# Softmax of phi taken where its tokens lie along a row, and brought to rows by way of DRAM

## The chip, the cores and the metric

One core of one Trainium2 chip. The metric is device microseconds of the whole program, inputs and output in DRAM. The five engines that the profile names are PE (TensorE; PEld is its weight load), DVE (VectorE), ACT (ScalarE), POOL (GpSimd) and SP (SyncE), which here only issues transfers.

## The reference

Attention through 32 memory slots per head, and behind it a mixer with a product over tokens and one over channels. Eight batches, eight heads, 576 tokens, 64 channels per head, 32 slots.

```python
# attention: q, k, v (8, 8, 576, 64), phi (8, 8, 576, 32)
a = np.exp(phi - np.max(phi, axis=2, keepdims=True))       # over the 576 tokens
a = a / (np.sum(a, axis=2, keepdims=True) + 1e-09)
k_m = np.einsum('bhsm,bhsd->bhmd', a, k)
v_m = np.einsum('bhsm,bhsd->bhmd', a, v)
scores = np.matmul(q, k_m.transpose(0, 1, 3, 2)) / np.sqrt(64)
scores = scores - np.max(scores, axis=-1, keepdims=True)    # over the 32 slots
attn = np.exp(scores)
attn = attn / (np.sum(attn, axis=-1, keepdims=True) + 1e-09)
x = np.matmul(attn, v_m)                                    # to (8, 576, 512)
# mixer: w_tok1 (576, 256), w_tok2 (256, 576), w_ch1 (512, 1536), w_ch2 (1536, 512)
u = x + (np.maximum(x.transpose(0, 2, 1) @ w_tok1, 0) @ w_tok2).transpose(0, 2, 1)
out = u + np.maximum(u @ w_ch1, 0) @ w_ch2
```

## The kernel before

Products whose result must stay exact split each float32 operand into a high and a low part and use three matmuls (high by high, high by low, low by high). ACT makes the high part with a copy, DVE or POOL the low part with a subtraction.

The work has two kinds of unit. A *quad* is four heads of one batch (16 of them, each attention and token mixing). A *chunk* is 512 tokens of u, through both channel products (cp and acc in the rows). The first three chunks are taken straight from PSUM; the u of later tokens is spilled to DRAM and done at the end in pairs of chunks with fewer products of sums.

The program runs in three stages, which the trace shows: to about 120 us the weights are converted and the first quads done, from 120 to 372 us the quads of batches 2 to 7 with chunks 1 and 2 between them, from 372 us the pairs. The stage in the middle is ordered by a planner: every step of every quad is entered with its engine, an estimated duration, the buffers that it takes and the steps that it waits for, and beside it stands a table of ranks, `PLACES`, one number for each step, that says which step goes first where several could. `plan` walks through this and writes one order, in which the instructions then stand on each engine. Its three numbers in the call (slack, margin, behind) and the due times in `do(...)` shape it too. The order of the last stage is written out in code.

Eleven quads, (2,1) to (7,1), are of the class `LateQuad`. In the kernel before, one goes like this. `load_turned` brings phi with a partition for each head and slot and the tokens along the row (288 KB). `phi_max` (L637) takes the largest of each row and turns these 128 numbers with a small transpose; `max_out` (L642) puts them into DRAM. `load_phi` (L621) brings phi a second time, now with a partition for each token (320 KB, padded to 640 columns); `max_in` (L648) reads the maxima back, spread over all partitions (tile r). `phi_sub` (L652) subtracts them on POOL, and `phi_only_exp` (L443) takes the exponential on ACT. `get_kv` (L662) calls `step_kv` (L446): 40 matmuls of phi by keys and values into the tile kvp, 130 columns each, since k and v carry a column of ones for the sums. `scales` (L665) adds 1e-9 to that column and takes the reciprocal. Then `spread_T`, `turn_T`, `get_kb` make the keys ready, and `scores` (rows with L490) needs them and q (L631). Softmax over slots follows; S goes to DRAM and comes back by rows (L542, then L552 and L554, tiles rows and side), is multiplied with the token weights (Ap), split into Ah and Al (L741, L745), multiplied with v (Rp, L753), and the result gives u (L772). ACT copies u to the tile side (L782), SP spills it (L800).

SP takes its instructions in order and issues nearly all transfers; a transfer whose buffer isn't free or whose data isn't there holds up all behind it. Of the rooms that matter there are one each for kv and q, two for phi and two for the turned phi, so the next quad's q can be issued only when the scores before have read the old one.

Beside the quads, the middle stage makes sums of weights for the pairs (L316, L317, L320), reads back the u of the first spilled chunks (tile u_p, L207) and makes its parts (L274, L278: xphi, xS, xkv), and adds up o, the residual of a chunk, on POOL (L179), which is stored to out (L188).

Of the kernel before, what the change touches and what calls it, by code (L numbers as in the profile page):

```python
# [28 lines left out]
def kernel(  # L29
# [20 lines left out]
    B, _, _, _, NC, _, D1 = kv.shape  # L50
    D = D1 - 1
# [369 lines left out]
    def kv_room(name):  # L421
        t = sb.tile([P, 2624], F32, tag="kv", name=name, bufs=1)[:, : 2 * NC * 4 * D1]
        return t.rearrange("p (z j i d) -> p z j i d", z=2, j=NC, i=4)

    class Quad:
        def __init__(s, b, Q):
            s.b, s.Q, s.n = b, Q, f"_{b}_{Q}"

# [28 lines left out]

        def scales(s):
            s.ms = wp.tile([P, 6], F32, tag="ms", name="ms" + s.n, bufs=1)
            sm = wp.tile([P, 1], F32, tag="ps", name="ps" + s.n, bufs=3)  # L460
            nc.vector.tensor_scalar_add(out=sm, in0=s.kvp[:, D:D1], scalar1=1e-9)
            nc.vector.reciprocal(out=sm, in_=sm)
            nc.vector.tensor_scalar_mul(out=s.ms, in0=mask[:, :6], scalar1=sm)
            s.per = sm

        def double_T(s):

            s.T = sb.tile([P, 2, D], F32, tag="pr", name="T" + s.n, bufs=2)
            nc.vector.tensor_scalar_mul(
                out=s.T, in0=s.kvp[:, :D].unsqueeze(1).to_broadcast([P, 2, D]), scalar1=s.per  # L470
            )
# [2093 lines left out]
```

## Time and profile before

| | |
|---|---|
| median of 3 runs | 721.87 us (721.57 to 722.58) |
| profiled execution | 722.28 us, of which its span is 720.4 us |
| PE, DVE, ACT, POOL busy in the span | 706.0, 519.6, 370.4, 82.6 us |
| mean granted clock of TensorE | 0.998 |
| DMA | 155.26 MB, 216 GB/s over the span; written to HBM 37.16 MB |
| chain that ended last | PE 89%, DMA 5%, DVE 3%, ACT 1%, issue 1% |

The busy times overlap: they are shares of one span. The chain is what stood between the start and the last instruction, step by step; an engine's share of it is what would shorten the run at once if it went. The granted clock is in parts of full speed.

### The profile page before, as it was taken

Reading aid. Unit: us, or ns where it says so; the run is one execution under the profiler, and the core shown is the slowest. Engines: PE = TensorE matmul, PEld = TensorE weight load, DVE = VectorE, ACT = ScalarE, POOL = GpSimd, SP = SyncE. Lnnn points to the kernel's source line nnn. Section 1 sums busy time; section 2 is a strip of 40 time slices with the busy share of each in tenths; the row PEclk is TensorE's granted clock in tenths of the full one; section 3 lists DMA queues with packets and bytes.
Section 4 is the critical chain, followed back from the end, with each engine's and each line's share of the span. In section 5 each row is a group of like instructions: output and inputs, shape, how many; then the busy total and the mean of one; then the engine's idle time right before and its main releaser. Section 6 shows DMA issues by size and latency. Waiting matters only on the chain.

```text
span 720.4 us, 11496 instructions
## 1 busy us (share of the span) xinstructions
PE 706.0 (98%) x4305; PEld 589.9 (82%) x4305; DVE 519.6 (72%) x857; ACT 370.4 (51%) x686; POOL 82.6 (11%) x79
## 2 busy tenths in 40 slices
PE   8899999999999989999999999999999999999998
PEld 8678888778888858888878888888888888888887
DVE  5999974887767877579785758966247977426983
ACT  6899774334545435554643465434345443436450
POOL 2132114111201411211400000000000000000000
PEclk9999999999999999999999999999999999999999
DMA  9975431988677998855726886185659064668302
GB/s 358 415 294 212 147 123 44 327 291 290 211 234 228 324 317 266 328 175 161 247 66 236 285 281 247 36 300 160 203 167 331 31 221 162 203 202 279 102 29 88
DMA packets 65503, 155.26 MB, mean 216 GB/s; under 512 B 10536, under 2 KB 28584, under 8 KB 61096
## 3 DMA queue, kind: packets, MB, share of 16 engines
q1 hardware_dynamic: 54936, 121.37, 47.9%
q10 hardware_dynamic: 10512, 33.17, 14.4%
q8 instruction: 34, 0.56, 0.3%
q14 instruction: 21, 0.17, 0.1%
HBM read 117.34 MB, written 37.16 MB: 214 GB/s over the span
## 4 chain that ended last, share of the span: by engine, by line
PE 89%; DMA 5%; DVE 3%; ACT 1%; issue 1%; SPq 0%; ACTq 0%; DVEq 0%
PE ma L291 14%; PE cp L145 13%; PE acc L168 12%; PE mU L2347 10%; PE mB L2347 7%; PE mc L291 7%; PE u L772 7%; PE mD L2347 3%; PE mA L2347 3%; PE mb L291 3%; PE Ap L572 3%; DMA raww<-in_w_tok_dram 2%; PE kvp L450 2%; DMA spilled<-side 2%; DMA side<-rows 1%; PE u L588 1%
## 5 line engine op out<-in xcount | busy, mean ns | idle before, releaser
L168 PE MATMUL acc<-hh,c 128*128 128x512 f32 x288 | 102.7, 401 | 0.0
L168 PEld LDWEIGHTS acc<-hh,c 128*128 128x128 f32 x288 | 54.6, 190 | 15.0 <-issue 4.2
L168 PE MATMUL acc<-hl,c 128*128 128x512 f32 x144 | 56.7, 394 | 0.0
L145 PE MATMUL cp<-uh,c1h 128*128 128x512 f32 x144 | 51.8, 400 | 0.0
L145 PE MATMUL cp<-ul,c1h 128*128 128x512 f32 x144 | 50.4, 391 | 0.0
L145 PE MATMUL cp<-uh,c1l 128*128 128x512 f32 x144 | 50.4, 391 | 0.0
L2333 ACT CAST rT<-hid 128x512 fp32r<-128x512 f32 x54 | 32.0, 621 | 26.8 <-PE mB L2347 15.6
L2334 DVE TENSOR_TENSOR rT<-hid,rT 128x512 fp32r<-128x512 f32 x54 | 35.6, 683 | 7.0 <-ACT rT L2333 7.0
L2201 DVE TENSOR_TENSOR hid<-mb,hid 128x512 f32<-128x512 f32 x12 | 8.3, 692 | 41.8 <-ACT hid L2281 41.8
L118 DVE SCALAR_TENSOR_TENSOR hl<-cp,hh 128x512 fp32r<-128x512 f32 x36 | 24.7, 686 | 18.1 <-ACT hh L115 18.1
L115 ACT ACTIVATE hh<-cp 128x512 fp32r<-128x512 f32 x36 | 21.6, 599 | 27.0 <-PE cp L145 26.5
L715 POOL TENSOR_TENSOR nat<-side,nat 128x512 fp32r<-128x512 f32 (+1 forms) x24 | 21.9, 911 | 98.2 <-ACT nat L706 72.5
L2204 ACT ACTIVATE hid<-hid 128x512 f32<-128x512 f32 x24 | 15.2, 632 | 34.8 <-DVE hid L2201 34.8
L145 PEld LDWEIGHTS cp<-uh,c1h 128*128 128x128 f32 x144 | 26.7, 188 | 6.4 <-issue 1.5
L145 PEld LDWEIGHTS cp<-uh,c1l 128*128 128x128 f32 x144 | 27.0, 188 | 5.9
L145 PEld LDWEIGHTS cp<-ul,c1h 128*128 128x128 f32 x144 | 27.1, 188 | 4.9
L168 PEld LDWEIGHTS acc<-hl,c 128*128 128x128 f32 x144 | 27.4, 190 | 4.1
L2333 ACT CAST r<-hid 128x512 fp32r<-128x512 f32 x36 | 22.4, 623 | 14.8 <-PE mU L2347 5.4
L2334 DVE TENSOR_TENSOR r<-hid,r 128x512 fp32r<-128x512 f32 x36 | 24.7, 685 | 4.5 <-ACT r L2333 4.2
L653 POOL TENSOR_TENSOR phi<-phi,r 128x640 f32<-128x640 f32 x11 | 17.8, 1617 | 86.4 <-DMA r<-top 70.5
L772 PE MATMUL u<-w2h,Rh 128*128 128x288 f32 x96 | 27.2, 298 | 0.3 <-ACT side L782 0.3
L291 PE MATMUL ma<-xrest_p,unit 128*128 128x512 f32 x108 | 27.4, 389 | 0.0
(380 smaller groups left out, 1914.7 us busy)
## 6 DMA issues: line engine op xcount, KB each, us to landing
unit<-sums ACTq DMA_DIRECT2D x54, 512.0 KB, 6.1
kv<-in_kv_dram SPq DMA_DIRECT2D x12, 1300.0 KB, 7.7
rawc<-in_w_ch_dram SPq DMA_DIRECT2D x12, 1024.0 KB, 8.2
q<-in_q_dram SPq DMA_DIRECT2D x16, 576.0 KB, 5.9
sums<-sums SPq DMA_DIRECT2D x12, 512.0 KB, 7.3
u_p<-spilled SPq DMA_DIRECT2D x6, 1024.0 KB
phi<-in_phi_dram SPq DMA_DIRECT2D x16, 320.0 KB, 3.4
unit<-sums ACTq DMA_DIRECT2D x18, 256.0 KB, 4.1
```

Of the source, the lines that this page charges most:

```text
L115: nc.scalar.activation(out=h, in_=ps, func=AF.Relu)
L118: nc.vector.scalar_tensor_tensor(out=l, in0=ps, scalar=0.0, in1=f32(h), op0=ALU.max, op1=ALU.subtract)
L145: nc.tensor.matmul(ps, l[:, a], r[:, a], start=n == 0, stop=n == len(mm) - 1)
L168: nc.tensor.matmul(ps, l_[f // 2][:, f % 2, a * P : (a + 1) * P], r[:, w], start=f == start and x == 0, stop=f == end - 1 and x == 2,)
L291: nc.tensor.matmul(ps, l, r, start=first and n == 0, stop=n == len(mm) - 1, skip_group_check=not first,)
L572: nc.tensor.matmul(ps[:, :TT], a, w, start=x == 0, stop=x == len(mm) - 1)
L653: eng.tensor_tensor(out=s.pt, in0=s.pt, in1=s.r.rearrange("p (i m) -> p i m", i=4) .unsqueeze(2) .to_broadcast([P, 4, NC, M]), op=ALU.subt ...
L715: eng.tensor_tensor(out=o, in0=a, in1=f32(h), op=ALU.subtract)
L772: nc.tensor.matmul(s.up[db, hf][:, :HALF], a, r, start=x == 0, stop=x == len(mm) - 1)
L2333: nc.scalar.copy(out=t[:, 0], in_=x)
L2334: nc.vector.tensor_tensor(out=t[:, 1], in0=x, in1=f32(t[:, 0]), op=ALU.subtract)
L2347: nc.tensor.matmul(s.banks[room][a][:, w], l_[:, a * P : a * P + P], r_, start=not (p or x) and name in ("11", "T1", "21", "T4"), stop=p = ...
```

## The change

For the eleven late quads phi is now loaded once, in the turned form, and the softmax is taken there. `phi_max` takes the largest of each row and negates it (one DVE instruction, no transpose). `phi_exp` on ACT takes the exponential with that number as its bias, and sums each row as it goes. `scales` adds 1e-9 to the sum and takes the reciprocal, now ahead of the product. `phi_turn` transposes the 128x576 tile on DVE in blocks of 32x32, `phi_out` puts it into DRAM (tile turns), `phi_in` brings it back with a partition for each token, in six transfers, in the way the rows of S come back (four of 64 KB, two of 16 KB). `get_kv` now uses 128 columns, takes the 64 tokens of the rest first, and kv has no column of ones (1,280 KB for 1,300). The second load of phi, the trip of the maxima and the subtraction on POOL are gone. On the host, tokens are laid out so that the blocks of 32 end at the right partitions. The table of ranks and the three numbers of the call are others, and so are the due times of these steps; the order of the whole middle stage changes with that.

```diff
-        t = sb.tile([P, 2624], F32, tag="kv", name=name, bufs=1)[:, : 2 * NC * 4 * D1]
+        t = sb.tile([P, 2624], F32, tag="kv", name=name, bufs=1)[:, : 2 * NC * 4 * D]
...
-        def phi_only_exp(s):
-            nc.scalar.activation(out=s.pt, in_=s.pt, func=AF.Exp)
-
-        def step_kv(s, ps=None):
-            s.kvp = bank([P, CW], "kvp" + s.n) if ps is None else ps
-            for j in range(NC):
-                for i in range(4):
-                    nc.tensor.matmul(
-                        s.kvp[32 * i : 32 * i + 32, : 2 * D1],
-                        s.pt[:, i, j, :],
-                        s.kv[:, :, j, i, :],
-                        start=j == 0,
-                        stop=j == NC - 1,
-                    )
...
-        def take_rows(s, t):
-            n, by_token = FULL * P, s.rows.rearrange("(i t) n -> t i n", t=32)
+        def by_rows(s, rows, t):
+            n, by_token = FULL * P, rows.rearrange("(i t) n -> t i n", t=32)
             main = t[:, :n].rearrange("p (i n) -> p i n", i=4)
             last = t[:TAIL, n:].rearrange("p (i m) -> p i m", i=4)
             for g in range(4):
@@ -554,6 +519,10 @@
                 nc.sync.dma_start(
                     out=last[32 * g : 32 * g + 32], in_=by_token[:, :, n + M * g : n + M * g + M]
                 )
+            return main, last
+
+        def take_rows(s, t):
+            main, last = s.by_rows(s.rows, t)
...
         def phi_max(s):
-            t = s.turned
-            nc.vector.tensor_reduce(out=t[:, :1], in_=t, axis=AX.X, op=ALU.max)
-            nc.vector.transpose(out=t[:, M : 2 * M], in_=t[:, :M])
-
-        def max_out(s):
-            s.top = dram.tile([1, 4 * M], F32, name="top" + s.n, tag="maxima", bufs=4)
-            nc.sync.dma_start(
-                out=s.top.rearrange("a (i m) -> (a i) m", m=M), in_=s.turned[:: P // 4, M : 2 * M]
-            )
-
-        def max_in(s):
-            s.r = sb.tile([P, 4 * M], F32, tag="pr", name="r" + s.n, bufs=2)
-            nc.sync.dma_start(out=s.r, in_=s.top.to_broadcast([P, 4 * M]))
-
-        def phi_sub(s, eng):
-            eng.tensor_tensor(
-                out=s.pt,
-                in0=s.pt,
-                in1=s.r.rearrange("p (i m) -> p i m", i=4)
-                .unsqueeze(2)
-                .to_broadcast([P, 4, NC, M]),
-                op=ALU.subtract,
-            )
+            s.col = wp.tile([P, 2], F32, tag="ps", name="col" + s.n, bufs=3)
+            nc.vector.tensor_reduce(out=s.col[:, :1], in_=s.turned, axis=AX.X, op=ALU.max, negate=True)
+
+        def phi_exp(s):
+            nc.scalar.activation(
+                out=s.turned, in_=s.turned, func=AF.Exp, bias=s.col[:, :1], accum_out=s.col[:, 1:]
+            )
+
+        def scales(s):
+            s.per = s.col[:, 1:]
+            nc.vector.tensor_scalar_add(out=s.per, in0=s.per, scalar1=1e-9)
+            nc.vector.reciprocal(out=s.per, in_=s.per)
+
+        def phi_turn(s):
+            s.pt = sb.tile([P, 4 * M * NC], F32, tag="phi", name="phi" + s.n, bufs=2)
+            nc.vector.transpose(out=s.pt[:, :S], in_=s.turned)
+
+        def phi_out(s):
+            s.turns = dram.tile([P, S], F32, name="turns" + s.n, tag="turns", bufs=2)
+            nc.sync.dma_start(out=s.turns, in_=s.pt[:, :S])
+
+        def phi_in(s):
+            s.pm, s.pl = s.by_rows(s.turns, s.pt)
 
         def get_kv(s):
-            s.step_kv(pch.tile([P, CW], F32, tag="ch", name="kvp" + s.n, bufs=2))
-
-        def scales(s):
-            s.per = wp.tile([P, 1], F32, tag="ps", name="ps" + s.n, bufs=3)
-            nc.vector.tensor_scalar_add(out=s.per, in0=s.kvp[:, D:D1], scalar1=1e-9)
-            nc.vector.reciprocal(out=s.per, in_=s.per)
+            s.kvp = pch.tile([P, CW], F32, tag="ch", name="kvp" + s.n, bufs=2)
+            for j in (FULL, *range(FULL)):
+                for i in range(4):
+                    own = s.pm[:, i, M * j : M * j + M] if j < FULL else s.pl[:, i]
+                    nc.tensor.matmul(
+                        s.kvp[M * i : M * i + M, : 2 * D], own, s.kv[: own.shape[0], :, j, i, :],
+                        start=j == FULL, stop=j == FULL - 1,
+                    )
 
         def vb_room(s, room):
             s.vb = side[0][:, 640:896] if room.tag[0] == "s" else sb.tile([P, 256], F32, tag="vb", name="vb" + s.n, bufs=1)
 
         def spread_v(s, room):
             s.vb_room(room)
-            EarlyQuad.spread_values(s, s.vb, s.kvp[:, D1 : D1 + D])
+            EarlyQuad.spread_values(s, s.vb, s.kvp[:, D : 2 * D])
...
-    ahead = [(quads[1, 0].x_u[3].end, late[1].load_turned)] + [(118.0, fn) for fn in (late[1].phi_max, late[1].max_out)]
+    ahead = [(quads[1, 0].x_u[3].end, late[1].load_turned)] + [(118.0, late[1].phi_max)]
...
-            turned = room("al", 2)
+            turned, col = room("al", 2), room("ps", 3)
             y = qd.l_turned = do(TURN_AT, "SP", 0.45, qd.load_turned, begin, take=[turned], move=0.81)
-            y = do(-38, "DVE", 0.85, qd.phi_max, y, use=[turned])
-            y = do(-37, "SP", 0.45, qd.max_out, y, use=[turned], move=0.02)
-            y.lands = True
-        z = do(-32, "SP", 0.45, qd.load_phi, begin, take=[phi_room], move=0.9)
-        r = room("pr", 2)
-        y = do(-30, "SP", 0.45, qd.max_in, y, z, take=[r], move=0.24)
-        z = do(-23, *PHI_SUB(qd), y, z, use=[phi_room, r], port=True)
-        e = do(-22, "ACT", 0.8, qd.phi_only_exp, z, use=[phi_room])
-        e.cushion = 2.0 * CUSHION
+            y = do(-40, "DVE", 0.72, qd.phi_max, y, take=[col], use=[turned])
+        z = do(-38, "ACT", 0.8, qd.phi_exp, y, use=[turned, col])
+        qd.scaled, qd.colr = do(-36, "DVE", 0.36, qd.scales, z, use=[col]), col
+        z = do(-37, "DVE", 0.8, qd.phi_turn, z, take=[phi_room], use=[turned])
+        z = do(-36, "SP", 0.45, qd.phi_out, z, use=[phi_room], move=0.81)
+        z.lands = True
+        e = do(-30, "SP", 2.8, qd.phi_in, z, use=[phi_room], move=1.18)
...
-            z = do(-8, "DVE", 0.32, qd.scales, z, take=[per], use=[bk])
-            y = do(-8, "ACT", 0.37, qd.spread_T, z, take=[T], use=[bk, per])
...
-        869, 851, 904, 880, 898, 895, 868, 813, 879, 909, 907, 897, 889, 886, 890, 863, 783, 821, 876, 885,
...
+        838, 841, 885, 859, 842, 883, 890, 856, 903, 833, 839, 900, 887, 860, 873, 877, 823, 812, 827, 829,
...
-    order = plan(dict(zip(steps, PLACES, strict=True)), dict.fromkeys(steps, 0), 0.4117, 3.2087, 4.7083)
+    order = plan(dict(zip(steps, PLACES, strict=True)), dict.fromkeys(steps, 0), 0.4013, 2.6573, 5.2164)
...
-    whole = phi.reshape(B, 4, 2, S, M).transpose(0, 2, 1, 4, 3).reshape(B, 2, P, S)
+    by_block = np.arange(S)
+    by_block[:n] = by_block[:n].reshape(4, P // 4, j).transpose(0, 2, 1).ravel()
+    whole = phi[:, :, by_block].reshape(B, 4, 2, S, M).transpose(0, 2, 1, 4, 3).reshape(B, 2, P, S)
     arrays = dict(
         q=np.concatenate([early[:1], late[1:]]),
-        kv=ones(np.stack([rows(k, 0), rows(v, 0)], axis=3).transpose(0, 1, 2, 3, 5, 4, 6)),
-        phi=planned(rows_phi, turned.reshape(rows_phi.shape)),
+        kv=np.stack([rows(k, 0), rows(v, 0)], axis=3).transpose(0, 1, 2, 3, 5, 4, 6),
+        phi=turned.reshape(rows_phi.shape)[:3],
```

Where the instructions of the middle stage stand is shown at two places. The first is SP, about 250 us into the kernel before. In the kernel before, the rows from the maxima of one late quad to kv of a later one; `spilled_105` and `spilled_106` are the two parts of a quad's spill, `u_p` the read back of spilled tokens, `out_dram` the store of a finished chunk, `q_0_3004` the q of quad (6,0).

```order
L644 DMA top_1_2883<-phiT_1_2725 4x32
L623 DMA phi_1_2895<-in_phi_dram 128x640
L635 DMA phiT_0_2899<-in_phi_turned_dram 128x576
L207 DMA u_p_2924<-spilled_104 128x2048
L188 DMA out_dram<-o_2806 128x2048
L800 DMA spilled_105<-side 128x2x256
L800 DMA spilled_106<-side 128x2x320
L650 DMA r_1_2975<-top_1_2883 128x128
L631 DMA q_0_3004<-in_q_dram 128x1152
L623 DMA phi_0_3009<-in_phi_dram 128x640
L627 DMA kv_1_3014<-in_kv_dram 128x2600
```

Here u_p, the store, the spills and two loads of phi stand between two loads of q. After the change the spill, the store and u_p stand as follows, on SP, from the spill of quad (4,0) on; `turns` is the turned exponential in DRAM, `sums` the sums of weights.

```order
L767 DMA spilled_105<-side 128x2x256
L767 DMA spilled_106<-side 128x2x320
L187 DMA out_dram<-o_2817 128x2048
L517 DMA phi_1_2779<-turns_1_2867 32x4x128 x4
L519 DMA phi_1_2779<-turns_1_2867 32x4x32 x2
L378 DMA sums_1380<-sums_2938 128x1024 x2
L592 DMA kv_1_3074<-in_kv_dram 128x2560
L385 DMA sums_1381<-c1h_1133 128x512
L385 DMA sums_1381<-c1h_1133 128x256
L385 DMA sums_1381<-c1l_1134 128x512
L385 DMA sums_1381<-c1l_1134 128x256
L206 DMA u_p_3143<-spilled_104 128x2048
```

The store to out comes behind the spills, u_p nine rows further down, and between them stand a phi on its way back, kv and the sums. The rows right behind them, to the kv of quad (7,0):

```order
L507 DMA rows_1_3178<-S_1_2892 128x576
L622 DMA turns_0_3182<-phi_0_3163 128x576
L600 DMA phiT_1_3191<-in_phi_turned_dram 128x576
L767 DMA spilled_105<-side 128x2x256
L767 DMA spilled_106<-side 128x2x320
L378 DMA sums_1381<-sums_3140 128x1024 x2
L596 DMA q_1_3288<-in_q_dram 128x1152
L517 DMA phi_0_3163<-turns_0_3182 32x4x128 x4
L519 DMA phi_0_3163<-turns_0_3182 32x4x32 x2
L592 DMA kv_0_3330<-in_kv_dram 128x2560
```

The way out of `phi_0_3163` stands second here and its way back eighth, with five rows between them; the q between them is that of quad (6,1). The other place is DVE near the last late quad, (7,1). Before, from the low part of a hidden tile of chunk 2 to its Al:

```order
L118 SCALAR_TENSOR_TENSOR hl_2_4115<-cp_2_4079,hh_2_4114 128x512
L320 TENSOR_TENSOR cw_4048<-cw_4048,ch_4049 128x1024
L278 TENSOR_TENSOR xS_p_4164<-u_p_2924,xphi_p_4162 128x512
L278 TENSOR_TENSOR xkv_p_4161<-u_p_2924,xphi_p_4163 128x512
L726 TENSOR_TENSOR a_7_1_4177<-aT_1_4006,a_7_1_4177 64x576
L726 TENSOR_TENSOR a_7_1_4178<-aT_1_4006,a_7_1_4178 64x576
L745 TENSOR_TENSOR Al_1_4208<-Ap_1_4180,Ah_1_4203 128x256
```

The low half of a sum of weights (`cw`, L320) stands ahead of xS and xkv, and two low parts of a (L726) ahead of Al. After the change, on DVE, from the same low half (now L319) to the same Al (`Al_1`, now L712):

```order
L319 TENSOR_TENSOR cw_3982<-cw_3982,ch_3983 128x1024
L712 TENSOR_TENSOR Al_0_4102<-Ap_0_4078,Ah_0_4100 128x256
L117 SCALAR_TENSOR_TENSOR Rl_0_4127<-Rp_0_4109,Rh_0_4119 128x512
L117 SCALAR_TENSOR_TENSOR hl_2_4135<-cp_2_4096,hh_2_4134 128x512
L277 TENSOR_TENSOR xS_p_4183<-u_p_3143,xphi_p_4181 128x512
L277 TENSOR_TENSOR xkv_p_4180<-u_p_3143,xphi_p_4182 128x512
L693 TENSOR_TENSOR a_7_1_4202<-aT_1_4053,a_7_1_4202 64x576
L693 TENSOR_TENSOR a_7_1_4203<-aT_1_4053,a_7_1_4203 64x576
L712 TENSOR_TENSOR Al_1_4234<-Ap_1_4205,Ah_1_4229 128x256
```

The sum's low half now stands ahead of the Al of the quad before, `Al_0`; xS, xkv and the two low parts still stand ahead of `Al_1`.

## Rows read from the trace of the kernel before

**Rows 1.** The page, part 1: busy us, share of span, instructions by engine.

```profile
PE 706.0 (98%) x4305; PEld 589.9 (82%) x4305; DVE 519.6 (72%) x857; ACT 370.4 (51%) x686; POOL 82.6 (11%) x79
```

**Rows 2.** Waits of PE, 120 to 372 us: us in all, times, longest.

```profile
PE sp L490 <- DMA q<-in_q_dram: 3.4, 1, 3.4
PE Rp L753 <- DVE Al L745: 2.3, 1, 2.3
```

**Rows 3.** Timeline of PE, 266 to 276 us: start, us, what, idle before it.

```profile
268.35 1.22 PE L490 MATMUL sp<-q,kb 64*32 64x288 f32 x16 [3.44 <-DMA q<-in_q_dram]
...
272.70 0.29 PE L772 MATMUL u<-w2h,Rh 128*128 128x288 f32 x1
...
275.30 0.40 PE L772 MATMUL u<-w2h,Rh 128*128 128x288 f32 x1 [0.32 <-ACT side L782]
```

**Rows 4.** Timeline of SP, 248 to 258 us.

```profile
250.90 0.50 SPq L644 DMA_DIRECT2D top<-phiT  x1
...
256.84 0.82 SPq L631 DMA_DIRECT2D q<-in_q_dram  x1
```

**Rows 5.** Stretches: PE, PEld, DVE, ACT, POOL busy, granted clock, DMA share, GB/s.

```profile
230.00:300.00 70.00, 66.08 (x542) 55.02 (x545) 50.71 (x90) 34.53 (x79) 17.22 (x15) 0.98 0.93 311
250.00:290.00 40.00, 36.24 (x285) 29.76 (x285) 28.16 (x54) 19.37 (x43) 8.38 (x8) 0.96 0.87 279
290.00:300.00 10.00, 10.00 (x101) 8.51 (x103) 5.71 (x9) 5.60 (x13) 0.00 (x0) 1.00 1.01 389
```

**Rows 6.** Chain of waits, 236 to 372 us: start, us, what.

```profile
287.85 4.24 PE u L772 x32
...
292.09 1.68 PE Ap L572 x14
...
298.61 0.65 PE sp L490 x16
299.25 1.25 PE kvp L450 x40
...
310.18 0.71 PE Rp L753 x6
...
320.81 2.72 PE cp L145 x12
```

**Rows 7.** Timeline of all engines, 351.9 to 362.5 us.

```profile
351.99 0.40 ACT L782 COPY side<-u 128x288 f32<-128x288 f32 x1 [0.38 <-PE u L772]
...
353.09 6.93 POOL L179 TENSOR_TENSOR o<-uh,ul 128x512 f32<-128x512 f32 x4
...
353.23 1.14 ACT L274 CAST xphi_p<-u_p 128x512 fp32r<-128x512 f32 x2
...
353.37 2.10 DVE L320 TENSOR_TENSOR cw<-cw,ch 128x1024 fp32r<-128x1024 f32 x1 [2.17 <-ACT ch L317]
...
355.39 1.78 DVE L278 TENSOR_TENSOR xS_p<-u_p,xphi_p 128x512 fp32r<-128x512 f32 x1
...
358.91 2.51 DVE L726 TENSOR_TENSOR a<-aT,a 64x576 fp32r<-64x576 f32 x2
...
359.26 0.40 PE L753 MATMUL Rp<-vl,Ah 128*128 128x256 f32 x2
...
361.46 0.42 DVE L745 TENSOR_TENSOR Al<-Ap,Ah 128x256 fp32r<-128x256 f32 x1
```

**Rows 8.** Tile u_p, on DVE: ns min/median/max, first and last start.

```profile
L278 DVE TENSOR_TENSOR xS_p<-u_p,xphi_p x3: 684/685/1784, 355.4 to 589.3; 128x512 fp32r<-128x512 f32 x3
```

**Rows 9.** Costliest lines, 120 to 372 us: busy us, mean ns, idle before.

```profile
L653 POOL TENSOR_TENSOR phi<-phi,r 128x640 f32<-128x640 f32 x11 | 17.8, 1617 | 86.4 <-DMA r<-top 70.5 <-DMA phi<-in_phi_dram 8.3 <-DMA sums<-c1h 7.7
...
L527 DVE STREAM_TRANSPOSE aT<-S 128x576 f32<-128x576 f32 x12 | 9.3, 777 | 0.3
```

**Rows 10.** Tile S, 120 to 372 us: from its DMAs' issue to landing.

```profile
DMA to landing us min/median/max: 2.5/5.8/7.8
```

**Rows 11.** Timeline of SP, 140 to 345 us, a return of rows.

```profile
147.14 1.75 SPq L552 DMA_DIRECT2D side<-rows  x4
```

More of the change, by code (lines that the diff above doesn't have):

```diff
@@ L49 @@
     )
-    B, _, _, _, NC, _, D1 = kv.shape
-    D = D1 - 1
+    B, _, _, _, NC, _, D = kv.shape
     M = phi.shape[5]
@@ L427, in __init__ @@
             s.b, s.Q, s.n = b, Q, f"_{b}_{Q}"
-        def load_phi(s):
-            s.pt = sb.tile([P, 4, NC, M], F32, tag="phi", name="phi" + s.n, bufs=2)
-            nc.sync.dma_start(out=s.pt, in_=phi[s.b, s.Q])
         def load_kv(s):
@@ L441, in load_q @@
             nc.sync.dma_start(out=s.qT.rearrange("p i n -> p (i n)"), in_=q[s.b, s.Q])
-        def phi_only_exp(s):
-            nc.scalar.activation(out=s.pt, in_=s.pt, func=AF.Exp)
-        def step_kv(s, ps=None):
-            s.kvp = bank([P, CW], "kvp" + s.n) if ps is None else ps
-            for j in range(NC):
-                for i in range(4):
-                    nc.tensor.matmul(
-                        s.kvp[32 * i : 32 * i + 32, : 2 * D1],
-                        s.pt[:, i, j, :],
-                        s.kv[:, :, j, i, :],
-                        start=j == 0,
-                        stop=j == NC - 1,
-                    )
-        def scales(s):
[L459 to L470, printed above, removed]
-            )
         def v_high(s):
@@ L619, in __init__ @@
             s.b, s.Q, s.n, s.up = b, Q, f"_{b}_{Q}", {}
-        def load_phi(s):
-            s.pt = sb.tile([P, 4, NC, M], F32, tag="phi", name="phi" + s.n, bufs=2)
-            nc.sync.dma_start(out=s.pt, in_=phi[s.b, s.Q])
         def load_kv(s):
@@ L652, in phi_sub @@
-        def phi_sub(s, eng):
-            eng.tensor_tensor(
-                out=s.pt,
-                in0=s.pt,
-                in1=s.r.rearrange("p (i m) -> p i m", i=4)
-                .unsqueeze(2)
-                .to_broadcast([P, 4, NC, M]),
-                op=ALU.subtract,
-            )
-        def get_kv(s):
-            s.step_kv(pch.tile([P, CW], F32, tag="ch", name="kvp" + s.n, bufs=2))
-        def scales(s):
-            s.per = wp.tile([P, 1], F32, tag="ps", name="ps" + s.n, bufs=3)
-            nc.vector.tensor_scalar_add(out=s.per, in0=s.kvp[:, D:D1], scalar1=1e-9)
-            nc.vector.reciprocal(out=s.per, in_=s.per)
+            s.col = wp.tile([P, 2], F32, tag="ps", name="col" + s.n, bufs=3)
@@ L1254, in mm_half @@
                     nc.tensor.matmul(
-                        to[m], s.pt[:, j, m], s.half[z][:, j, i, :D], start=j == 0, stop=j == NC - 1
+                        to[m], s.pt[:, j, m], s.half[z][:, j, i], start=j == 0, stop=j == NC - 1
                     )
@@ L1265, in load_half @@
                     s.wide = t
-                t = t[:, : NC * 4 * D1]
+                t = t[:, : NC * 4 * D]
                 s.half.append(t.rearrange("p (j i d) -> p j i d", j=NC, i=4))
@@ L1496, in mm_kv @@
                     nc.tensor.matmul(
-                        s.kvp[m, : 2 * D], s.pt[:, j, m], s.kv[:, :, j, i, :D],
+                        s.kvp[m, : 2 * D], s.pt[:, j, m], s.kv[:, :, j, i],
                         start=j == 0, stop=j == NC - 1,
@@ L1828 @@
     kv2, q2, pt2 = room("kv"), room("qT"), room("aT")
-    turned1 = room("al", 2)
+    turned1, col1 = room("al", 2), room("ps", 3)
     begin = step(
         "END", 0, None,
-        take=[*sum(c1_rooms, []), *u_rooms[1], o_rooms[0], rest_room, *hidden[0, NF - 1], kv2, q2, pt2, turned1],
+        take=[*sum(c1_rooms, []), *u_rooms[1], o_rooms[0], rest_room, *hidden[0, NF - 1], kv2, q2, pt2, turned1, col1],
     )
@@ L1866 @@
     SUMS_AT = [10, 35, 60, 85, 110, 135]
-    PHI_ON, LOW_ON, O_ON = "POOL", "POOL", "POOL"
+    LOW_ON, O_ON = "POOL", "POOL"
     CUSHION = 0.9
     O_AT = 0
-    def PHI_SUB(qd):
-        return PHI_ON, 1.75 if PHI_ON == "POOL" else 0.95, lambda: qd.phi_sub(engines[PHI_ON])
     def NAT_LOW(qd):
@@ L1916 @@
         bk, kb, vh, vl, vb = bank_rooms[n], kb_rooms[n], vh_rooms[n], vl_rooms[n], Room(("side vb", 1), ("vb", 1))
-        T, per = room("kb") if n else room("pr", 2), room("ps", 3)
+        T = room("kb") if n else room("pr", 2)
         z = got_kv
         if n:
-            z = do(-8, "DVE", 0.32, qd.scales, z, take=[per], use=[bk])
-            y = do(-8, "ACT", 0.37, qd.spread_T, z, take=[T], use=[bk, per])
+            y = do(-8, "ACT", 0.37, qd.spread_T, z, qd.scaled, take=[T], use=[bk, qd.colr])
         else:
             y = do(-8, "DVE", 0.35, qd.spread_T, z, take=[T], use=[bk])
-        v = do(-8, "DVE", 0.48, lambda qd=qd, r=vb: qd.spread_v(r), *([z] if n else [z, y]), sided, take=[vb], use=[bk, side_room, per])
+        v = do(-8, "DVE", 0.48, lambda qd=qd, r=vb: qd.spread_v(r), z, qd.scaled if n else y, sided, take=[vb], use=[bk, side_room] + [qd.colr] * (n > 0))
         y = do(-7, "PE", 0.12, qd.turn_T, y, v, use=[bk, T])
@@ L2497, in rows @@
         return out
-    def ones(x):
-        out = np.ones((*x.shape[:-1], x.shape[-1] + 1), x.dtype)
-        out[..., :-1] = x
-        return out
-    def planned(x, turned):
-        return np.concatenate([turned[:2], np.stack([turned[2, 0], x[2, 1]])[None], x[3:]])
     def words(x):
```

2 lines of the change are left out of this document (1 added, 1 removed), and 94 rows, old and new, of the table PLACES.

## Prediction

> **What bounds the kernel now.** I read the page first. TensorE (PE) is busy 98% of the span [rows 1], so time can change only where PE waits, where its clock falls, or where its own work changes. I then asked who PE waits for between 120 and 372 us, the stretch in which the late quads run and which alone is planned anew. Two waits stand out [rows 2]: 3.4 us of the scores for a q transfer, 2.3 us of the R product for Al from VectorE (DVE). The timeline shows a third of 0.32 us behind the first [rows 3].
>
> The first wait comes from the SP queue. From 250.90 us SP issues nine transfers, one after the other: a top, phi, phiT, u_p, out, two spills, r and then the q that is waited for; the first and the last stand in [rows 4]. Their sizes by the order (128x2048 words of 4 bytes are 1,024 KB) add up to 3,872 KB. PE gets its q at 268.35 us [rows 3], 17.45 us after the burst's first issue: 222 KB/us. Over 230 to 300 us the DMA engines move 311 GB/s (304 KB/us), over 250 to 290 us 279 GB/s (272 KB/us) at a busy share of 0.87 [rows 5]. So here the queue, not a single transfer, is the limit. The clock pays too: from 268.35 to 272.70 us PE does 16 scores (0.65) and 12 matmuls of acc (2.72 us for 12 such at full rate, [rows 6]), 3.37 us of work in 4.35: 0.98 lost, with the granted clock at 0.96 over that stage [rows 5].
>
> The second wait is DVE's [rows 7]. It does the low half of a weight sum (L320) to 355.47, then xS, xkv, two a_low, and only then Al, which PE wants from 359.66 (the end of its last product with Ah); Al starts at 361.46. GpSimd (POOL) adds the residual (L179) all the while, to 360.02, and xS takes 1,784 ns where its median is 685 [rows 8].
>
> **The change part by part.** All of it is counted against the profiled execution, 722.28 us (span 720.4 and 1.88 around it); the median of the runs is 721.87, 0.41 less.
>
> *Keys and values product.* 128 columns instead of 130. Forty matmuls of 130 columns take 1.25 us [rows 6]; 2/130 of that, for 11 quads, is 0.2 us. Between 0, if a matmul's time doesn't follow its columns so finely, and that; I take **-0.2**.
>
> *Work off PE.* Per quad POOL loses one subtraction (1,617 ns), DVE loses a small transpose and gets one over 128x576 (like L527, 777 ns) [rows 9], and does the two scale operations earlier, after the exponential instead of after the product. ScalarE's exponential runs over 576 columns instead of 640 and also sums. DVE: at most 11 x 0.78 = 8.5 us more in the 252 us, of which it is busy about three quarters (50.7 of 70 us, [rows 5]). Neither of the two long PE waits ends on these instructions, and the scales leave the path between product and keys. What hides them is PE's own work of the quads ahead. **0**; if that cover fails at every quad, up to 8.5 us, and below zero at most the 0.3 of the third wait.
>
> *Transfers.* Per quad, before: phi 320, phiT 288, r 64, kv 1,300, together 1,972 KB. After: phiT 288, out to DRAM 288, back 288, kv 1,280: 2,144 KB, 9% more; 11 quads make 1.9 MB, 6 us of the queue at 304 KB/us, of which PE sees what comes late. SP issues nine instructions for five. The way out is like that of the attention's S, which lands after 2.5 to 7.8 us, median 5.8 [rows 10]; the way back is six pieces, like the attention's rows. The new order puts other entries between out and back, for quad (7,0) five rows of it, so only a full queue makes PE see the trip.
>
> *The burst.* In the new SP order u_p, out and the spills no longer stand together just ahead of a q: u_p comes nine rows behind out, and the q of (6,0), whose scores waited, goes out ahead of both. That wait goes with what follows it: 3.44 + 0.98 + 0.32 = **-4.7**.
>
> *What is late next.* The same queue. From the spill of quad (4,0) to the kv of quad (7,0), both in the new piece of the order, SP issues 10,592 KB. PE's work in that time, added up from the order with the durations of [rows 6], is 28 Ap (3.3 us), 87 cp and acc (19.7), 12 Rp (1.4), two kv products of 40 matmuls (2.5), 64 u (8.5), two groups of 16 scores (1.3) and two turns (0.2 at an Rp's price), together 36.9 us, of which 0.6 passes before the spill is issued (a copy of 0.40 and its start): 36.3. At 304 KB/us the queue needs 34.9 us and is in time by 1.4; at 272 it needs 38.9 and is late by 2.6; at 222, the pace of the burst, 47.7 and late by 11.4. The bounds are 0 and 11.4. I take **+1.5**, between the two stage rates and nearer to that of 250 to 290 us, in which the same kinds of transfers run.
>
> *The Al wait.* In the new order L320's successor (L319) stands ahead of the Al of the quad before, so xS need not wait for it, nor its cast for that sum's. With the u copy over at 352.39, half of the xphi cast (0.57) lets xS start near 353.1 instead of 355.39; xS and xkv take 3.5, the two a_low 2.51 here, the second after the residual's end, and some 3.1 if it lasts through both; Al's 0.42 then ends near 360.2. But the new order also has one group of three acc matmuls less ahead of Ap (0.68 us), so PE wants Al at 359.0: a wait of about 1.2 is left of 2.3. **-1.1**, between 0 and -2.3. What slows DVE here is the residual, which stays. The Trainium skill (GPSIMD Engine Reference, Key points) says that GpSimd shares its SBUF interfaces with VectorE and contends with instructions that read two SBUF inputs; rows 8 agree (1,784 against 685 ns). By that rule alone, with POOL's 11 subtractions gone, one could hope for the whole 2.3, 1.2 us less than my sum.
>
> Sum: -0.2 + 0 - 4.7 + 1.5 - 1.1 = -4.5, so 717.8 for a run like the profiled one, and **717.3** for the median.
>
> **The rivals.** *1. The waits only move.* For it: with a queue at 0.93 busy [rows 5] the new order, with more bytes, can make a q or kv late elsewhere by as much as it saves. Against: between the scores that free q's room and the next that need it there are 9.9 us of PE work at the tightest, about as before. Only -0.2 is left: 721.7.
>
> *2. The queue is slower with more small pieces.* Four pieces take SP 1.75 us to issue [rows 11], so the six of one return about 2.6 for 288 KB; at 304 KB/us their bytes need 0.95. If the queue runs at the pace of issue, each return costs 1.7 us more, two of them in the stretch 3.4: 720.7. Against: while such pieces are in it, the stretch of 290 to 300 us moved 389 GB/s, with its share at 1.01 [rows 5]. The Trainium skill (DMA: Bandwidth & Descriptors, Bandwidth) has a 64 KB transfer at 138 GB/s, which it measured on another issuing path; by an estimate from that figure a return would need 2.1 us. No row here shows one return alone.
>
> *3. Slower: the queue falls to the pace of the burst.* The kv of (7,0) comes 11.4 us late, and the clock falls as it did (1.0). Place: scores of (6,1) and product of (7,0). 717.3 - 1.5 + 11.4 + 1.0 = 728.2. For it: the one measured burst ran at 222. Against: that burst held 2,048 KB of u_p and out, one of them a store; the whole stage ran at 272. It decides below about 255 KB/us, where the lateness with its clock reaches the 6.0 us that the other terms give.
>
> **How the numbers follow.** The measurement of this kernel can tell 0.2% from no change, 1.4 us: faster is below 720.4, slower above 723.3. The forecast, with the queue between 0 and 3 us late, holds 0.62: all faster (715 to 719.5). Rival 1 has 0.13 and rival 2 0.08: the same, 0.21 together. Rival 3, with milder forms of it, 0.17. The low end, 714.6, is the sum with no lateness (-1.5) and the Al wait gone (-1.2). The high end, 724.5, leaves out the worse half of rival 3.
>
> **What would show it.** Right: no PE wait on q near 268 us; a granted clock of 1.00 from 260 to 280; PE waiting 0.5 to 1.5 us for Al near the last R; POOL's busy time down by some 17.8 us [rows 9]; HBM written up by about 3.2 MB (11 x 288 KB); any new wait on a DMA (kv or phi) or on a copy behind a spill between 265 and 300 us. Wrong: a wait for phi's return before a product earlier than that, which says the trip through DRAM is not covered; a wait of PE on ACT or DVE at one of the early quads, which says that the moved exponential and transpose cost what I put at nothing; a PE wait on kv over 6 us, rival 3.

## The result

The change makes the kernel slower: 732.89 us (median of 6 runs, 730.81 to 734.15) against 722.23 us before, a ratio of 1.0139 with a 95% interval of 1.0119 to 1.0160. 717.3 us was forecast. The ratios below are each against runs of the kernel before on the same chip, where its median was up to 723.7 us, so kernels are compared by their ratios; 0.01 is 7.2 us.

The page of the changed kernel, parts 1 and 4, beside [rows 1]: PE's busy share fell by a point, and of the chain that ended last 14% are now transfers and 2% SP's own issuing, which had 5% and 0%.

```profile
PE 710.5 (97%) x4305; PEld 588.9 (80%) x4305; DVE 522.2 (71%) x857; ACT 372.1 (51%) x697; POOL 65.1 (9%) x68
...
PE 78%; DMA 14%; DVE 4%; SPq 2%; ACT 1%; issue 1%; ACTq 0%; DVEq 0%
```

The waits of PE in the middle stage, 120 to 385 us, beside [rows 2] (us in all, times, longest):

```profile
PE u L739 <- ACT side L749: 4.8, 3, 2.6
PE kvp L632 <- DMA kv<-in_kv_dram: 2.5, 3, 1.3
PE Rp L720 <- DVE Al L712: 2.4, 3, 1.0
PE kvp L632 <- issue: 1.6, 1, 1.6
PE kvp L649 <- DVE col L613: 1.1, 1, 1.1
PE u L739 <- DVE col L613: 0.5, 1, 0.5
PE pp L1109 <- DVE ul L193: 0.3, 1, 0.3
```

No wait for q is left, but 13.2 us of others are there, none over 2.6 us, nearly all from 166 us on; the kernel before had 6.5 in this stage, 5.7 of them in two waits. Most have a transfer behind them: kv that came late, or the spilled side that could not be left, or rows of S that had not come back. Of the other 5.3 of the 12.0 us by which the span grew, 4.5 are PE busy for longer. The granted clock doesn't explain that: from 240 to 300 us it is 0.97 in the change (below) and was 0.97 before as well.

One of the waits for kv, and then that window in the kernel before:

```profile
222.62 1.43 PE L632 MATMUL kvp<-kv,phi 64*32 64x128 f32 x40 [1.32 <-DMA kv<-in_kv_dram]
```

```profile
240.00:300.00 60.00, 56.08 (x449) 47.00 (x445) 43.32 (x79) 30.09 (x69) 14.87 (x13) 0.97 0.92 307
```

Who held up the transfers? SP's timeline in the changed kernel, around 200 us (start, us, what):

```profile
194.13 0.53 SPq L622 DMA_DIRECT2D turns<-phi  x1
195.04 0.33 SPq L507 DMA_DIRECT2D rows<-S  x1
195.73 0.37 SPq L767 DMA_DIRECT2D spilled<-side  x1
202.32 2.20 SPq L517 DMA_DIRECT2D phi<-turns  x4
204.57 0.91 SPq L519 DMA_DIRECT2D phi<-turns  x2
205.58 1.80 SPq L517 DMA_DIRECT2D side<-rows  x4
207.78 0.78 SPq L519 DMA_DIRECT2D side<-rows  x2
208.66 0.43 SPq L596 DMA_DIRECT2D q<-in_q_dram  x1
...
212.73 1.00 SPq L592 DMA_DIRECT2D kv<-in_kv_dram  x1
```

SP waits until the turned phi has landed in DRAM (202.32), then issues twelve pieces, six of phi and six of S, 576 KB in 6.2 us. That is 92 KB/us, a third of the stage's rate. The kv behind them goes out at 212.73 and is waited for at 222.6. The DMA engines meanwhile run dry, as the windows of the changed kernel show (PE, PEld, DVE, ACT, POOL, granted clock, DMA share, GB/s):

```profile
240.00:300.00 60.00, 53.36 (x413) 43.26 (x415) 44.29 (x81) 26.86 (x65) 9.03 (x8) 0.97 0.88 284
205.00:210.00 5.00, 5.00 (x37) 4.87 (x36) 4.64 (x11) 2.08 (x6) 0.00 (x0) 1.00 0.47 95
```

A share of 0.47 is what a queue short of work looks like, not one that is full.

### The profile page after: what moved, and what is told of

It is laid out like the page before. It is cut to its first block, busy times and chain, and to the rows that moved or that the text cites. A ratio compares the mean times of both kernels' runs of the same rounds, so it can differ in the third digit from the quotient of the medians.

```text
span 732.4 us, 11570 instructions
## 1 busy us (share of the span) xinstructions
PE 710.5 (97%) x4305; PEld 588.9 (80%) x4305; DVE 522.2 (71%) x857; ACT 372.1 (51%) x697; POOL 65.1 (9%) x68
## 3 DMA queue, kind: packets, MB, share of 16 engines
q10 hardware_dynamic: 10512, 33.17, 14.4%
## 4 chain that ended last, share of the span: by engine, by line
PE 78%; DMA 14%; DVE 4%; SPq 2%; ACT 1%; issue 1%; ACTq 0%; DVEq 0%
PE ma L290 13%; PE acc L167 10%; PE mU L2308 10%; PE cp L144 9%; PE mc L290 7%; PE mB L2308 7%; PE u L739 4%; DMA kv<-in_kv_dram 4%; PE mD L2308 3%; PE mb L290 3%; PE mA L2308 3%; DMA rows<-S 2%; DMA phiT<-in_phi_turned_dram 2%; DMA raww<-in_w_tok_dram 2%; PE Ap L541 2%; DMA side<-rows 1%
## 5 line engine op out<-in xcount | busy, mean ns | idle before, releaser
L167 PE MATMUL acc<-hh,c 128*128 128x512 f32 x288 | 100.1, 397 | 0.0
L167 PEld LDWEIGHTS acc<-hh,c 128*128 128x128 f32 x288 | 54.1, 188 | 14.4 <-issue 3.3
L749 ACT COPY side<-u 128x288 f32<-128x288 f32 (+1 forms) x44 | 16.9, 390 | 21.7 <-PE u L739 18.1
```

Source lines behind the costliest of these rows:

```text
L167: nc.tensor.matmul(ps, l_[f // 2][:, f % 2, a * P : (a + 1) * P], r[:, w], start=f == start and x == 0, stop=f == end - 1 and x == 2,)
L749: nc.scalar.copy(out=side[0][:, o + n : o + HALF], in_=ps[:, n:HALF])
```

## The experiments

Theories: A, the trip through DRAM makes the kernel late; B, the new order does, whatever the trip costs. Within A: the pieces (A1), the bytes or the wait for the way out (A2); and then, within the pieces, SP's time (P1), their number in flight (P2), or their short rows (D).

| kernel | transfers of the trip per quad | median us | ratio to before, 95% |
|---|---|---|---|
| the change | 1 + 6 | 732.9 | 1.0139 (1.0119 to 1.0160) |
| no trip | 0 | 716.3 | 0.9913 (0.9891 to 0.9935) |
| one piece | 1 + 1 | 717.9 | 0.9925 (0.9899 to 0.9951) |
| from the input | 0 + 6 | 722.8 | 0.9998 (0.9971 to 1.0024) |
| on POOL's queue | 1 + 6 | 736.3 | 1.0187 (1.0153 to 1.0221) |
| six, long rows | 1 + 6 | 730.9 | 1.0112 (1.0082 to 1.0141) |
| three, short rows | 1 + 3 | 723.4 | 0.9997 (0.9979 to 1.0015) |
| two and two | 2 + 2 | 722.8 | 0.9996 (0.9977 to 1.0014) |
| two and two, S too | 2 + 2 | 716.7 | 0.9916 (0.9889 to 0.9943) |
| one piece, five tiny | 1 + 1 + 5 | 727.2 | 1.0046 (1.0029 to 1.0064) |
| one piece, SP held | 1 + 1 | 725.6 | 1.0022 (1.0004 to 1.0040) |
| before, S two and two | (none) | 719.6 | 0.9936 (0.9917 to 0.9955) |

**No trip.** 

> The changed kernel without the trip through DRAM: phi_out and phi_in issue nothing, and the product reads the turned tile as it lies, so the keys and values are mixed wrongly; all else keeps its place in the order. Theory A (the trip's load on SP and on the DMA engines makes the kernel late): below 721 us, most of the 10.7 us back, and the waits on kv and on side gone. Rival B (the new order of the middle is worse by itself, whatever the trip costs): 730 us or more, with the same waits.

```diff
-            nc.sync.dma_start(out=s.turns, in_=s.pt[:, :S])
...
-            s.pm, s.pl = s.by_rows(s.turns, s.pt)
+            n = FULL * P
+            s.pm = s.pt[:, :n].rearrange("p (i n) -> p i n", i=4)
+            s.pl = s.pt[:TAIL, : 4 * M].rearrange("p (i m) -> p i m", i=4)
```

The ratio is 0.9913: the order and all else of the change are worth 6.3 us, and B falls. All waits of PE in the middle stage that are left:

```profile
PE Rp L721 <- DVE Al L713: 0.7, 1, 0.7
PE pp L1110 <- DVE ul L193: 0.3, 1, 0.3
```

**One piece.** 

> The changed kernel with the way back as one transfer of 128x576 words in place of six pieces: the same 288 KB, the same wait for the way out, but 1 issue on SP for 6 (0.44 us each, so 2.2 us of SP less per quad) and long rows in place of rows of 512 bytes. It brings phi back unsorted, so the keys and values are mixed wrongly. Theory A1 (the pieces are what costs: SP's issue time, in which the DMA engines run dry, or the short rows): 722 to 727 us. A2 (bytes, or SP's wait for the way out): within 1.5 us of 732.9. Rival B (the order): 732.9.

```diff
-            s.pm, s.pl = s.by_rows(s.turns, s.pt)
+            nc.sync.dma_start(out=s.pt[:, :S], in_=s.turns)
...
```

The same bytes, the same wait for the way out, and the ratio is 0.9925: 0.0214 less than the change, 15.5 us (the two intervals allow some 2.4 us either way). The expectation of 722 to 727 was too high. Bytes and the wait for landing together cost 0.0012, which is not told from zero: A2 falls. Its window beside that of the change above: the same 60 us with more bytes and no slow clock.

```profile
240.00:300.00 60.00, 58.93 (x478) 48.50 (x477) 44.75 (x81) 29.62 (x70) 6.88 (x8) 1.00 0.93 327
```

And SP's own waits, first in the one-piece kernel, then in the change (120 to 330 us):

```profile
SPq L596 <- PE sp L455: 12.5, 5, 3.4
```

```profile
SPq L517 <- DMA rows<-S: 9.4, 3, 4.3
SPq L517 <- DMA turns<-phi: 9.3, 5, 6.1
SPq L517 <- DMA q<-in_q_dram: 6.8, 5, 2.2
SPq L596 <- DMA kv<-in_kv_dram: 5.5, 2, 2.8
SPq L385 <- DMA kv<-in_kv_dram: 4.3, 2, 2.3
...
SPq L596 <- PE sp L455: 2.9, 1, 2.9
```

With one piece SP is ahead: it waits 12.5 us for the scores to free q's room. In the change it waits for that only once. Most of its waits there are on transfers, also on ones that the waiting instruction doesn't read: L596 loads q and waits for kv. The trace says why, as each of SP's instructions names the semaphore that it waits for: from 120 to 330 us every transfer on SP takes the next of eight semaphores, and in the change none starts before the one eight places before it has landed. This is the program's doing, and it holds in all kernels here.

**From the input.** 

> The changed kernel with nothing sent out, and the six pieces read from the input in DRAM in place of the turned exponentials (raw phi in the product in place of its exponential). The issue of the pieces stays, the way out (288 KB) goes, and the way back waits for the transpose on DVE but no longer for a transfer to land. A1 (the pieces' issue): 730 us or more. A2 with SP's wait for the landing as the cause: 720 to 724. Bytes alone as the cause: half of the gain of the kernel without the trip. Rival B: 732.9.

```diff
-            nc.sync.dma_start(out=s.turns, in_=s.pt[:, :S])
...
-            s.pm, s.pl = s.by_rows(s.turns, s.pt)
+            s.pm, s.pl = s.by_rows(phi_turned[s.b - 2, s.Q], s.pt)
```

0.9998, between the two: without the wait and the way out, six pieces cost 0.0085 over no trip (6 us); with both, 0.0226. The pieces' cost is larger where SP has just waited. The figure expected from the pieces alone (730 or more) was too high, that of the landing wait (720 to 724) fits, and bytes alone (half of the gain without the trip, 724.6) would be near too. But the one-piece kernel has that wait and those bytes and loses nothing by them, so it is the pair of pieces and wait that costs.

**On POOL's queue.** 

> The changed kernel with both ways of the trip issued by POOL in place of SP; bytes, pieces and all other instructions stay. If SP's time is the cause (its issues, or its waits for the way out to land): 720 to 726 us, unless the low parts of nat on POOL, which now stand behind waiting transfers, come late. If the bytes on the DMA engines are the cause: within 1.5 us of 732.9.

```diff
-            nc.sync.dma_start(out=s.turns, in_=s.pt[:, :S])
+            nc.gpsimd.dma_start(out=s.turns, in_=s.pt[:, :S])
...
-            s.pm, s.pl = s.by_rows(s.turns, s.pt)
+            s.pm, s.pl = s.by_rows(s.turns, s.pt, nc.gpsimd)
```

1.0187, no test after all: the low parts of nat (the rows of S, split into high and low) stood behind the waiting pieces on POOL, as feared, and phi itself came late. Waits of PE, and then POOL's own (120 to 330 us):

```profile
PE kvp L632 <- DMA phi<-turns: 6.7, 2, 5.9
PE Ap L541 <- POOL nat L682: 6.1, 1, 6.1
```

```profile
POOL phi L517 <- issue: 41.5, 13, 7.0
POOL phi L517 <- DMA turns<-phi: 26.2, 6, 6.7
```

The Trainium skill (DMA: Bandwidth & Descriptors, Issuing engines are not separate DMA queues) says that issuing from several engines only saves the sequencer's time, which is usually small beside the transfer. Here the saving was eaten by POOL. From issue to landing a 64 KB piece takes 2.2 us in the change and its issue some 0.4, which agrees; but many in a row add up: four such pieces take SP 1.80 us above, and at the 304 KB/us of [rows 5] their bytes need 0.84.

**Six, long rows.** 

> The changed kernel with the way back as six transfers again, but by groups of partitions, with rows of 2,304 bytes (phi comes back unsorted, so keys and values are mixed wrongly). Theory P (SP's issue of the pieces, 0.44 us each, is the cost): near 733 us, as with the six short-rowed pieces. Theory D (the short rows are the cost, on the DMA engines): near 718, as with the one piece.

```diff
-            s.pm, s.pl = s.by_rows(s.turns, s.pt)
+            cuts = 0, 32, 64, 96, 112, 120, 128
+            for lo, hi in zip(cuts, cuts[1:]):
+                nc.sync.dma_start(out=s.pt[lo:hi, :S], in_=s.turns[lo:hi])
...
```

1.0112: 0.0187 over one piece with the same rows, 13.5 us. Short rows are at most the rest, 0.0027 (1.9 us), which the intervals don't tell from zero. D falls as the main cause.

**Three, short rows.** 

> The changed kernel with the four large pieces as one transfer whose rows are as short as theirs (512 bytes), and the two small ones as they are: three issues for six, the same bytes in the same rows (the blocks come back in wrong places, so keys and values are mixed wrongly). P: three of five saved issues' worth, near 724 us. D: 732.

```diff
-            s.pm, s.pl = s.by_rows(s.turns, s.pt)
+            n, by = FULL * P, s.turns.rearrange("(i t) n -> t i n", t=32)
...
+            nc.sync.dma_start(out=s.pm, in_=s.turns.rearrange("p (i n) -> p i n", i=4)[:, :, :P])
+            for g in range(2):
+                nc.sync.dma_start(out=s.pl[32 * g : 32 * g + 32], in_=by[:, :, n + M * g : n + M * g + M])
```

**Two and two.** 

> The changed kernel, computing all of the reference, with another place for each token: partition 4t+g in place of 32g+t, so that the rows of the way back lie at one stride and it takes two transfers (256 and 32 KB, rows of 512 and 128 bytes), and the way out two. Keys and values need nothing else than a host layout of phi with tokens in that order. Four issues for seven. P: near 724 us. D: 732, no gain.

```diff
...
+            nc.sync.dma_start(out=s.turns, in_=s.pt[:, :n])
+            nc.sync.dma_start(out=s.tails, in_=s.pt[:, n:S])
...
+            nc.sync.dma_start(out=s.pm, in_=s.turns.rearrange("(i t) (g n) -> (t g) i n", t=32, g=4))
+            nc.sync.dma_start(out=s.pl, in_=s.tails.rearrange("(i t) (g m) -> (t g) i m", t=32, g=2))
...
```

These two took 723.4 and 722.8 us, where 724 was expected of the number: four transfers per trip cost the same whether three of them come back or two. Two more than in the one-piece kernel cost 0.0072, 5.2 us; three more again (six, long rows) another 0.0115, 8.3 us.

**S too.** 

> The kernel with four issues for the trip of phi, and the same place of tokens for the attention's S (12 quads here, and 2 in the head): two out and two back in place of one and six; the token weights are laid out to fit. P: three more issues saved per quad, below the kernel with phi's alone by some 4 to 8 us, 716 to 720. D: no gain, 732.

 The same edit at `rows_out` and `by_rows`:

```diff
-            nc.sync.dma_start(out=s.rows, in_=s.S.rearrange("p a m -> p (a m)"))
...
+            nc.sync.dma_start(out=s.rows, in_=flat[:, :n])
+            nc.sync.dma_start(out=s.rest, in_=flat[:, n:])
...
+            nc.sync.dma_start(out=main, in_=rows.rearrange("(i t) (g n) -> (t g) i n", t=32, g=4))
+            nc.sync.dma_start(out=last, in_=rest.rearrange("(i t) (g m) -> (t g) i m", t=32, g=2))
...
```

0.9916: faster than both the kernel before and the change, and as good as having no trip at all, though it computes all of the reference.

**Five tiny** and **SP held.** 

> The kernel with the way back in one piece (phi unsorted, as there), and behind each of these eleven transfers five more that carry 16 bytes from a constant to DRAM, and that nobody reads: as many issues as with six pieces, hardly a byte more. If the number of transfers is what costs, whatever they carry: 729 to 733 us, as with the six long-rowed pieces. If it is bytes or rows on the DMA engines: 718.

 

> The kernel with the way back in one piece (phi unsorted, as there), and behind each of these eleven transfers 80 empty instructions on SP, so that SP is held for some 2 to 4 us per quad and no transfer is added. P1 (SP's time in issuing is the cost): 727 to 735 us, by how long they hold SP. P2 (the number of transfers is the cost and not SP's time: in the built program each transfer takes the next of eight semaphores and waits until the eighth transfer before it has landed, so six small pieces push six others out of this window): within 2 us of 717.9.

```diff
             nc.sync.dma_start(out=s.pt[:, :S], in_=s.turns)
+            for x in range(5):
+                t = dram.tile([1, 4], F32, name=f"tiny{x}" + s.n, tag="tiny", bufs=16)
+                nc.sync.dma_start(out=t, in_=mask[:1, :4])
...
```

```diff
             nc.sync.dma_start(out=s.pt[:, :S], in_=s.turns)
+            for x in range(80):
+                nc.sync.nop(hint="spin")
...
```

SP in the two, behind one way back:

```profile
200.98 0.32 SPq L625 DMA_DIRECT2D phi<-turns  x1
201.35 1.46 SPq L628 DMA_DIRECT2D tiny<-mask  x5
```

```profile
182.48 0.34 SPq L625 DMA_DIRECT2D phi<-turns  x1
185.79 0.81 SPq L385 DMA_DIRECT2D sums<-c1h  x2
```

The first pair of rows is of the tiny transfers, the second of the empty instructions, which the timeline doesn't list. Fifty-five transfers of 16 bytes cost 0.0121 over one piece, 8.7 us, though issuing a set takes SP 1.46 us only. Empty instructions that hold SP for 2.97 us (182.82 to 185.79) cost 0.0097, 7.0 us (in both the intervals allow some 2.3 us either way). So SP's time does cost, 7.0 us for 11 x 2.97 = 33 us held, 0.21 us for each; P2 alone falls. But by that price the tiny transfers would cost 11 x 1.46 x 0.21 = 3.4 us, and six long-rowed pieces for one (32.7 us of issuing over the eleven returns, against 5.0) 5.8; measured were 8.7 and 13.5. P1, as SP's issuing alone, falls too.

The rest, 5 to 8 us, goes with the number of transfers. The window of eight is a likely reason. Added up from the semaphores in the traces (120 to 330 us, one profiled run each), SP stood for the landing of the transfer eight places before for 29.0 us with one piece, 45.5 with the five tiny, 37.4 with six long rows, and 18.5 with SP held. Issuing and this wait together are then 32.5 us more with the tiny transfers, 36.2 with the six long rows and 22.2 with SP held, which cost 7.0, 0.32 for each. By that the tiny come to 10 us and the six to 11, which the intervals don't tell from 8.7 and 13.5. So SP's time, in issuing and in this window, is enough to account for both. No run changes the number of semaphores, so the window's share is worked out and not shown.

**Before, S two and two.** 

> The kernel before, computing all of the reference, with the attention's S out in two transfers and back in two in place of one and six, by the other place of tokens: three transfers fewer per quad, phi as it was. If the number of transfers is what makes q late in its burst too: the q wait (3.4 us) and what follows it shrink or go, 717 to 720 us. If that wait is of bytes alone: within 1.5 us of the kernel before.

 The edit is the one just shown, made in the kernel before. 0.9936, 4.6 us less. Its waits, the start of its burst on SP, the scores that wait for q and one window, beside [rows 2, 3, 4, 5]:

```profile
PE Rp L756 <- DVE Al L748: 2.3, 1, 2.3
PE sp L490 <- DMA q<-in_q_dram: 0.8, 1, 0.8
```

```profile
246.89 0.54 SPq L647 DMA_DIRECT2D top<-phiT  x1
```

```profile
265.74 0.72 PE L490 MATMUL sp<-q,kb 64*32 64x288 f32 x16 [0.85 <-DMA q<-in_q_dram]
```

```profile
250.00:290.00 40.00, 38.52 (x313) 32.45 (x312) 31.65 (x56) 21.60 (x48) 8.87 (x8) 1.00 0.97 338
```

The same 40 us that moved 279 GB/s move 338, with three transfers fewer per quad, so the rate that I had taken for the queue's limit was none of the DMA engines. The burst itself is not faster: from its first issue to the arrival of q it takes 18.85 us here and took 17.45 before. PE asks for q at 264.9 us in both; SP comes to the burst 4.0 us earlier.

This also says what the change is worth once S takes two and two in both kernels: 0.9916 with the change, 0.9936 without, a difference of 0.0020 (1.4 us) that the intervals don't tell from zero.

## Why the prediction was wrong

**The step that failed is "SP issues nine instructions for five", which the sum priced at nothing.** It counted the trip by its bytes (2,144 for 1,972 KB) and said that only a full queue makes PE see it. The bytes cost 0.0012 with the wait for landing; the six pieces cost 15.5 us. The term for what the queue makes late, +1.5 in the sum, measured 16.3 (the change against no trip, 0.0226). The rates of [rows 5] were used as the most that the queue can pass; with fewer transfers and no fewer bytes, such stretches moved 327 and 338 GB/s.

Most of the signs named for being right came all the same: no q wait, a granted clock of 1.00 from 260 to 280 us, 0.72 us for Al, POOL 17.5 us less busy, 3.24 MB more written to HBM. They belong to what the change saves; none of them tells how late the queue is.

**Rival 2 had the pieces, part of the mechanism and nearly the price.** It put 1.7 us on each return, and then counted two returns, those in the stretch in which lateness was expected, and gave it 0.08. Eleven returns at 1.7 are 18.7 us; 717.3 - 1.5 + 18.7 = 734.5, and 732.9 was measured. That this comes so near is partly luck: the pace of issue, which is all that it reckons with, gives 5.8 of the 13.5 us by the price above. The argument against it, that 290 to 300 us moved 389 GB/s with such pieces in it, misread the row: the pieces issued there landed 7.3 us later, and what moved had been issued before.

**Rival 3** had the sign and named the queue, but not the place. There is no wait of 11.4 us on the kv of (7,0); the lateness shows in most of a dozen waits of 0.3 to 2.6 us from 166 us on. Nor was 222 KB/us a pace of the queue: in the 17.45 us of that burst the DMA engines moved 307 GB/s (300 KB/us), so bytes issued before it were still under way.

```profile
250.90:268.35 17.45, 14.02 (x118) 11.02 (x118) 14.04 (x27) 6.45 (x15) 3.19 (x3) 1.00 0.90 307
```

**Keys and values product: -0.2 expected, +0.65 found.** Pieces of the chain in the kernel without the trip: seven of eleven products take 1.36 us, four 1.22, together 14.4, where eleven of the 1.25 of [rows 6] are 13.75.

```profile
165.74 1.36 PE kvp L633 x40
185.25 1.22 PE kvp L633 x40
```

**Work off PE: 0 expected.** So it is without the trip, where of the waits on ACT and DVE only Al's and one of 0.3 that was there before are left. In the change 1.1 us is a wait with `col` of L613 as its last releaser, and the timeline shows what lies behind:

```profile
238.44 0.75 DVE L604 TENSOR_REDUCE col<-phiT 128x1 f32<-128x576 f32 x1 [3.39 <-DMA phiT<-in_phi_turned_dram]
...
241.69 0.47 DVE L1118 SCALAR_TENSOR_TENSOR vb<-kvp,col,mask 128x256 f32<-128x256 f32 x1
```

The first step of the moved softmax, the maximum, waits on DVE for a phiT that SP issued late, and all that DVE has to do for the quad ahead, vb among it, stands behind it. I had counted what DVE does more, not what it waits for.

**The burst: -4.7 expected.** The q wait is gone in the change, but the slow clock has only moved: 0.83 from 280 to 290 us, where PE had waited 1.6 us until a kv landed (at 281.0). Without the trip both are gone, with a granted clock of 1.00 from 120 to 385 us. Taking three transfers per quad away shrinks the q wait to 0.8 in the order before too, though the burst's 3,872 KB take no less time there: what mattered was when SP came to them.

**The Al wait: -1.1 expected**, 1.2 us to be left; 0.72 is, so -1.6. The rows of the changed kernel that answer to [rows 7]:

```profile
366.56 6.48 POOL L178 TENSOR_TENSOR o<-uh,ul 128x512 f32<-128x512 f32 x4
...
367.45 0.94 DVE L277 TENSOR_TENSOR xS_p<-u_p,xphi_p 128x512 fp32r<-128x512 f32 x1 [2.80 <-ACT xphi_p L273]
368.32 1.78 DVE L277 TENSOR_TENSOR xkv_p<-u_p,xphi_p 128x512 fp32r<-128x512 f32 x1
...
370.31 3.34 DVE L693 TENSOR_TENSOR a<-aT,a 64x576 fp32r<-64x576 f32 x2 [0.21 <-ACT a L688]
...
373.68 0.42 DVE L712 TENSOR_TENSOR Al<-Ap,Ah 128x256 fp32r<-128x256 f32 x1
...
374.16 0.50 PE L720 MATMUL Rp<-vh,Al 128*128 128x256 f32 x2 [0.72 <-DVE Al L712]
```

As forecast, xS no longer waits for the weights' low half, and the residual still slows what stands beside it.

Without the term on the queue my sum was -6.0 us; the kernel without the trip measured -6.3 (the interval allows 1.6 either way). That the two agree so well is partly luck, as the product was off by +0.85 and the Al wait by -0.5.

## What to carry to other kernels

Count the transfers on an in-order queue, not only their bytes: each piece more per round cost about 2.6 us over eleven rounds here (5.2 for two, 13.5 for five), and the same bytes in one piece hardly anything. A price found for one instance is to be multiplied by all instances before the rival that it belongs to is given a small chance. A share of busy DMA engines near 0.9 doesn't say that bytes are the limit; take a transfer out and see whether the rate rises. And when an experiment finds a gain that the kernel before can have too, give it to that kernel as well before judging the change: here the difference then shrank to 0.0020.

## What the hardware showed that was not expected

Forty matmuls that begin with 64 rows cost 1.36 us behind matmuls of 128 rows and 1.22 behind the scores, which have 64 rows too. That is more than the two columns save. What takes the 0.14 us isn't shown: the kernel before goes from 128 to 64 rows inside its product, and there forty matmuls took 1.25 us behind both; no run tried the order of the rows by itself. And a transfer of 16 bytes held SP for 0.29 us (1.46 for five), not much less than one of 288 KB (0.32).
